# A gated mix of attention and a token MLP: the first layer's row work in a written order, other places in memory, another tail

## The chip, the core and the metric

The kernel runs on one core of a Trainium2 chip. Times are device microseconds of one launch. A core has five instruction streams that matter here: TensorE (PE, matmuls; its weight loads are counted apart as PEld), VectorE (DVE), ScalarE (ACT), GpSimd (POOL) and SyncE (SP, which issues most of the DMAs). Engines wait for each other by semaphores only; each of them runs its own instructions in order.

## The reference

The inputs are x (1 x 2048 x 512), the attention's weights, the weights and biases of a two-layer MLP that works across the tokens, and a gate's weights. All is in fp32.

```python
def _A_ref(x, wqkv, wo):                       # 32 heads of 16 columns
    qkv = (x @ wqkv).reshape(B, S, 3, H, Dh) ...
    scores = jnp.einsum("bhqd,bhkd->bhqk", q, k) * scale
    p = _softmax(scores, axis=-1)
    o = jnp.einsum("bhqk,bhkd->bhqd", p, v)
    return (o, heads side by side) @ wo

def _B_ref(x, w1, b1, w2, b2):
    h = _layernorm(x, axis=-1)                 # (B, S, D)
    u = _gelu(jnp.einsum("bsd,sf->bdf", h, w1) + b1)
    y = jnp.einsum("bdf,fs->bds", u, w2) + b2
    return y transposed to (B, S, D)

g = _sigmoid((x * gate_w).sum(-1, keepdims=True))
return g * _A_ref(x, wqkv, wo) + (1 - g) * _B_ref(x, w1, b1, w2, b2)
```

## The kernel before

Every fp32 operand of a matmul is split into two parts, hi and lo, in a faster matmul format (`split`, L65 and L66: a copy makes hi, a subtraction makes lo), and a product is three matmuls: hi with hi, hi with lo, lo with hi. Rows of x are taken in 16 chunks of 128, counted by c or t.

The work goes in these stages, in times of the profiled execution:

- To 53 us: x is loaded and turned (its transpose is kept as xt_hi and xt_lo), V and the gate are computed. The weights wv of V are four tiles, each with its hi and lo.
- To 145 us: the Q and K projections. Their split results go to DRAM as `qp` and `kp`. The first eight row chunks are normalised beside them (`ln_load`, `ln_scale`, `ln_rows`), which gives half 0 of h, `h_hi` and `h_lo` for c = 0 to 7.
- 145 to 306 us: the MLP's first layer (`layer`, L370). It has four passes over columns of w1, from f0 = 0, 512, 1024 and 1536; each of the first three fills four PSUM banks, the last fills two. In each pass, chunk after chunk, a weight block of 128 x 512 is loaded (`w_raw`, SP), split (`w_hi` on ACT, `w_lo` on POOL), and used by twelve matmuls. In the pass with f0 = 0, the layernorm of chunks 8 to 15 (half 1 of h) runs beside the first eight chunks. When a pass is done, its banks go through `gelu` (L378 to L383 and the split L65, L66), which uses the buffers `gu` and `gs` (two of each) and writes `u_hi` and `u_lo`.
- 307.6 to 314.5 us: the first 30 matmuls of the MLP's second layer (L696) into the bank `dn`.
- 314.6 to 1305.4 us: attention in 32 groups (two heads by half of the rows of Q each). A group's K and Q go by `load_k` into one of two fixed buffers, ks0 and ks1, and by `load_q` into `qs` (six and eight DMAs on SP, L424). Scores (L711) go to PSUM banks `s`, ACT exponentiates them (L720), and their products with V are summed in the bank `av` (L675). The rest of the second layer and most of the output projection are matmuls placed between these by a list written out by hand (L749). The four rows of each of K's buffers that carry a constant are filled once, by four memsets on DVE (L415).
- From 1305.4 us: the tail. The last group's output is divided by its softmax sums and goes into the projection of the last eight row chunks, and their rows are finished and stored.

Up to the attention a scheduler orders the instructions of each engine, by dependences and its own estimates, except in stretches under `manual_schedule`, where the order is that of the program. From the second layer's first matmul on, all engines are in program order.

Tiles lie in pools that are stacked from the left or the right side of SBUF. When a pool is closed, its bytes can be given out again; the first writer of the new tile then waits for the last reader of the old one. So where a pool stands in the stack decides who waits for whom. `k_bufs` (ks0, ks1) and `qs` are opened on the left after h and the first layer's pools have closed. PSUM has eight banks of 128 x 512 fp32: two for each of the three `s` buffers, one for `dn`, one for `av`.

Of the kernel before, what the change touches and what calls it, by code (L numbers as in the profile page):

```python
# [21 lines left out]
P = 128  # L22
# [36 lines left out]
def gated_mix(ctx: ExitStack, tc: tile.TileContext, a_x, a_wqkv, a_wo, b_w1, b_b1, b_w2, b_b2, gate_w, out):  # L59
# [81 lines left out]
    def weight():  # L141
        load_weight()
        split_weight()
        return ready.pop(0)
# [17 lines left out]
    with tc.tile_pool(name="vp", bufs=1, side="right") as pool:  # L162
# [104 lines left out]
    def ln_load(ln, c):  # L267
        xs[c] = ln.tile([P, D], F32, name="x")
        nc.sync.dma_start(xs[c], xf[c * P : (c + 1) * P, :])
        nc.vector.bn_stats(stats[:, c, :], xs[c])  # L270
        nc.vector.bn_aggr(mv[:, c, :], stats[:, c, :])

# [17 lines left out]
        split(h_hi[c], h_lo[c], hf, nc.scalar.copy, nc.vector.tensor_tensor)  # L290


    h_half(0)
    bd = h_ctx.enter_context(tc.tile_pool(name="bd", bufs=2))
    with tc.tile_pool(name="ln0", bufs=3, side="right") as ln:

# [17 lines left out]
        for b in range(ND):  # L314
# [9 lines left out]
            for n in range(NQ):  # L324
                ps = project(wq_b, n)
                parts(ps, qp_d[b], n, kmax[:, 0:1])
                greatest(qmax[:, n : n + 1], ps)
                if n % 2 and qk_cols:
                    qk_w.append(wcols(qk_cols.pop(0)))
                if n % 2 == 0:  # L330
                    c = 2 * b + n // 2
                    ln_load(ln, c)
                    ln_scale(ln, c, 1)
# [12 lines left out]
    def bring_most():  # L346
        nc.sync.dma_start(most_d, most)
        nc.sync.dma_start(most_row, most_d.rearrange("p b -> (p b)")[None, :])
# [23 lines left out]
    with tc.tile_pool(name="ln1", bufs=3, side="right") as ln, tc.tile_pool(name="gl", bufs=2, side="right") as gl:  # L372

        def gelu(ps, fb):
# [115 lines left out]

    end_ctx = ExitStack()
    end = sums_of = None
    rows = {}

    def open_end():
# [18 lines left out]
        slow.append((two + 5, lambda: split(wq[0], wq[1], raw, nc.vector.tensor_copy, nc.vector.tensor_tensor)))  # L514

    def fetch_o(half, k, pairs=4):

# [113 lines left out]

    two = 0

    def evacuate(g):
# [141 lines left out]
    with (  # L776
# [13 lines left out]
        sums, hi, lo = ([x.rearrange("p (i m c) -> p m i c", i=2, m=2)[:, m] for m in range(2)] for x in tiles)  # L790
        totals, last = (x.rearrange("p (i m c) -> p m i c", i=2, m=2) for x in (pa[7], last_ot))
        for m in range(2):
            nc.vector.tensor_scalar_max(sums[m], totals[:, m], LEAST_SUM)
        for m in range(2):
            nc.vector.reciprocal(sums[m], sums[m])  # L795
# [3 lines left out]
        behind = []  # L799
        for m in range(2):  # L800
            for i in range(2):
                for n, (a, b) in enumerate(((hi, 0), (hi, 1), (lo, 0))):
                    for j in range(4):
                        at = slice(32 * j, 32 * j + DH)
                        nc.tensor.matmul(pa[2 * j + m], a[m][at, i, :], wq[b][at, i, :], start=False, stop=i == 1 and n == 2)
            if m == 0:
                others(5, 7)
            for j in range(4):
                t = 2 * j + m
                row, gate, dst = rows[NH + t], g[:, NH + t : NH + t + 1], of[(NH + t) * P : (NH + t + 1) * P, :]  # L810
                if j == 1 or j == 3 and m == 0:
                    res = end.tile([P, D], F32, name=f"res{t}")
                    nc.scalar.activation(res, pa[t], AF.Copy, scale=gate)
                    nc.gpsimd.tensor_tensor(row, res, row, ALU.add)
                    behind.append((dst, row))
                else:
                    nc.vector.scalar_tensor_tensor(row, pa[t], gate, row, ALU.mult, ALU.add)
                    nc.sync.dma_start(dst, row)
        for dst, row in behind:
            nc.scalar.dma_start(dst, row)  # L820
    end_ctx.close()
    att_ctx.close()

# [79 lines left out]
```

## Time and profile before

| | |
|---|---|
| median of 3 runs | 1328.74 us (1327.55 to 1329.35) |
| the profiled execution's own time | 1328.09 us |
| its span, first to last instruction | 1326.2 us |
| mean granted TensorE clock | 0.997 |
| TensorE busy | 1309.7 us, 99% of the span |
| ACT busy | 1095.7 us, 83% |
| DVE busy | 414.3 us, 31% |
| GpSimd busy | 202.0 us, 15% |
| moved by DMA | 138.41 MB, 104 GB/s |

How to read it: the time runs from launch to end, the span from the first to the last instruction of the profiled execution, so 1.9 us lie outside the span. Busy shares are averages over stages with different limits. In the lines that follow, a tile's name stands for all of its buffers; "out<-in" names what an instruction writes and reads; Ln is a line of the kernel before; what stands in brackets is the idle time of the engine just before the instruction, and whom the profile takes to have ended it.

### The profile page before, as it was taken

The page shows a single profiled execution, that of the slowest core. Times are in us where ns is not written, and L with a number is a line of the kernel's source. Part 1 is how long each engine was busy: PE and PEld are TensorE (multiplying, and loading weights), DVE is VectorE, ACT ScalarE, POOL GpSimd, SP SyncE. Part 2 cuts the span into 40 slices and gives each one's busy share as a digit, 9 for nine tenths or more (in the row PEclk, how much of TensorE's full clock was granted, in tenths as well). Part 3 has the DMA queues.
Part 4 walks back from the last instruction along what each step waited for, and adds up shares of the span by engine and source line. Part 5 has one row for each costly group of instructions (what it writes and reads, how often), then busy time and mean ns, then how long its engine had stood idle before and what let it go on. Part 6 is the DMA issues. An engine that isn't in the chain of part 4 may idle for free.

```text
span 1326.2 us, 32411 instructions
## 1 busy us (share of the span) xinstructions
PE 1309.7 (99%) x13284; PEld 767.8 (58%) x13284; DVE 414.3 (31%) x626; ACT 1095.7 (83%) x1264; POOL 202.0 (15%) x468
## 2 busy tenths in 40 slices
PE   9999999999999999999999999999999999999996
PEld 7888878876555555555555555455554555545553
DVE  3596572445121111112422111232111112233224
ACT  3344343446999999999999999999999999999993
POOL 0210244442111111011100111100010101100001
PEclk9999999999999999999999999999999999999998
DMA  3588543328343333344555344544433433465411
GB/s 120 167 271 298 201 120 96 95 66 173 74 85 65 61 74 73 65 80 76 132 117 122 79 73 77 118 113 117 77 66 61 81 62 77 82 117 123 103 53 67
DMA packets 93385, 138.41 MB, mean 104 GB/s; under 512 B 14293, under 2 KB 53355, under 8 KB 90156
## 3 DMA queue, kind: packets, MB, share of 16 engines
q1 hardware_dynamic: 92796, 135.47, 43.4%
q8 instruction: 107, 1.75, 0.6%
q10 hardware_dynamic: 432, 0.79, 0.2%
q14 instruction: 50, 0.41, 0.1%
HBM read 99.63 MB, written 36.56 MB: 103 GB/s over the span
## 4 chain that ended last, share of the span: by engine, by line
PE 95%; DVE 2%; issue 1%; POOL 1%; ACT 0%; DMA 0%; SPq 0%; POOLq 0%; DVEq 0%
PE av L675 37%; PE s L711 28%; PE dn L749 10%; PE acc L73 10%; PE acc L370 9%; DVE ks L415 1%; PE dn L696 1%; PE acc L181 1%; POOL w_lo L66 1%; DMA wv_raw<-in_A_wqkv_dram 0%; DVE u_lo L66 0%; DVE sums L795 0%; DVE gs L381 0%; DVE gu L378 0%; ACT pt L720 0%
## 5 line engine op out<-in xcount | busy, mean ns | idle before, releaser
L720 ACT ACTIVATE pt<-s 128x1024 f32<-128x1024 f32 x1024 | 964.4, 1026 | 26.9 <-PE s L711 17.7
L711 PE MATMUL s<-qs,ks 64*128 64x512 f32 x2048 | 523.3, 420 | 0.5 <-ACT pt L720 0.4
L675 PE MATMUL av<-pt,v 128*17 128x256 f32 x8192 | 510.6, 381 | 0.0
L711 PEld LDWEIGHTS s<-qs,ks 64*128 64x128 f32 x2048 | 299.8, 184 | 205.6 <-ACT pt L720 179.0
L675 PEld LDWEIGHTS av<-pt,v 128*17 128x17 f32 x8192 | 205.2, 97 | 259.9 <-issue 119.5
L749 PE MATMUL dn<-u_hi,w_hi 64*128 64x512 f32 x428 | 182.1, 425 | 0.0
L66 POOL TENSOR_TENSOR w_lo<-w_raw,w_hi 128x512 fp32r<-128x512 f32 (+1 forms) x126 | 152.9, 1217 | 134.3 <-ACT w_hi L65 113.6
L749 PE MATMUL dn<-u_hi,w_lo 64*128 64x512 f32 x428 | 168.6, 394 | 0.0
L749 PE MATMUL dn<-u_lo,w_hi 64*128 64x512 f32 x428 | 168.6, 394 | 0.0
L753 POOL MEMSET token<- 1x1 f32 x320 | 30.3, 95 | 872.6 <-PE dn L749 666.4
L636 DVE COPY ot<-av 128x512 f32<-128x512 f32 x32 | 22.1, 692 | 355.2 <-PE av L675 348.6
L649 DVE RECIPROCAL rt<-rt 128x512 f32<-128x512 f32 x31 | 103.9, 3353 | 1.1
L370 PE MATMUL acc<-h_hi,w_lo 128*128 128x512 f32 x224 | 89.1, 398 | 1.9 <-POOL w_lo L66 1.8
L65 ACT CAST w_hi<-w_raw 128x512 fp32r<-128x512 f32 (+1 forms) x67 | 37.7, 565 | 64.0 <-PE acc L370 58.9
L370 PE MATMUL acc<-h_hi,w_hi 128*128 128x512 f32 x224 | 88.7, 396 | 0.4 <-ACT w_hi L65 0.4
L370 PE MATMUL acc<-h_lo,w_hi 128*128 128x512 f32 x224 | 88.5, 395 | 0.0
L749 PEld LDWEIGHTS dn<-u_hi,w_hi 64*128 64x128 f32 x428 | 78.8, 184 | 3.0
L749 PEld LDWEIGHTS dn<-u_lo,w_hi 64*128 64x128 f32 x428 | 79.2, 185 | 1.9
L749 PEld LDWEIGHTS dn<-u_hi,w_lo 64*128 64x128 f32 x428 | 79.0, 185 | 2.1
L65 DVE CAST w_hi<-w_raw 128x512 fp32r<-128x512 f32 (+1 forms) x61 | 22.4, 378 | 121.8 <-PE dn L749 59.6
L439 DVE TENSOR_SCALAR row<-dn,b2x,omg 128x512 f32<-128x512 f32 x16 | 13.0, 810 | 141.6 <-PE dn L749 133.2
L370 PEld LDWEIGHTS acc<-h_hi,w_lo 128*128 128x128 f32 x224 | 42.1, 188 | 14.1 <-POOL w_lo L66 4.1
(128 smaller groups left out, 1074.0 us busy)
## 6 DMA issues: line engine op xcount, KB each, us to landing
w_raw<-in_B_w_dram SPq DMA_DIRECT2D x96, 256.0 KB
ks<-kp SPq DMA_DIRECT2D x192, 128.0 KB
qs<-qp SPq DMA_DIRECT2D x256, 64.0 KB
qp<-pc SPq DMA_DIRECT2D x16, 768.0 KB
x<-in_A_x_dram SPq DMA_DIRECT2D x32, 256.0 KB
kp<-pc SPq DMA_DIRECT2D x16, 512.0 KB
w_raw<-in_B_w_dram SPq DMA_DIRECT2D x32, 128.0 KB
bp<-row SPq DMA_DIRECT2D x16, 256.0 KB
```

What stands on the lines that cost most here:

```text
L65: copy(hi, src)
L66: sub(lo, src, hi.bitcast(F32), ALU.subtract)
L73: nc.tensor.matmul(ps, a, b, start=start and n == 0, stop=stop and n == last)
L181: nc.tensor.transpose(pt[:, k, :], xs[t][:, k * P : (k + 1) * P], ident)
L370: nc.tensor.matmul(p, a, b, start=first and k == 0, stop=last and k == 2)
L636: nc.vector.tensor_copy(ot, av)
L649: nc.vector.reciprocal(rt, rt)
L675: nc.tensor.matmul(av[32 * j : 32 * j + VC, i * QC : (i + 1) * QC], v[:, c, g % NP * 2 + i, :], pt[:, h * QC : (h + 1) * QC], start=added[ ...
L711: nc.tensor.matmul(s[:, m, :], kt[grp][rows, c * P : (c + 1) * P], qt[grp][rows, qb * NB : (qb + 1) * NB], start=True, stop=True,)
L720: nc.scalar.activation(pt, s, AF.Exp, scale=SCALE)
L749: mm = nc.tensor.matmul(ps, a[half], b[half], start=first and not second, stop=last and bool(second))
L753: fence = nc.gpsimd.memset(token, 0.0)
```

## The change

Six things, in the order of the diff:

1. The hi and lo parts of three of the four wv tiles no longer have tiles of their own; they take the places of `w_hi` and `w_lo` (three buffers each), and the fourth takes two places of `w_raw`, which the first layer uses later.
2. `h_half` takes a side. h_lo lies ahead of h_hi in each half. Half 1 goes to the right side, below u, where it was on the left above half 0. What is opened on the right later (the x rows of the first layer and gu, gs) lies further down for it. By the compiled addresses, in bytes of a partition: half 1 of h from 118752 to 151520 (before: h_hi 87904 to 104288, h_lo 104288 to 120672); gu and gs from 95936 to 104128 (before: 132800 to 140992); ks0 from 89664 to 97856 and ks1 from 97856 to 106048 in both kernels.
3. The first pass of the first layer (f0 = 0) is under `manual_schedule` for ACT, DVE and GpSimd. `rows_beside(c)` writes out what goes beside chunk c: loads of x two chunks ahead (five buffers), the statistics of chunk 8 + c, for two chunks at a time the scale (`ln_scale` with n = 2, on odd c), and the rows of chunk 8 + c - 2.
4. The PSUM pools of attention are opened in another order: the three `s` buffers in banks 0 to 5, `dn` in 6, `av` in 7 (before: dn 0, av 1, s 2 to 7).
5. The last group's output is taken from `av` by two max operations with a value per partition, `least`, so that the sums can't be zero; the max against LEAST_SUM behind the sums' matmul goes.
6. In the tail, the sums are two matmuls of half the columns, the reciprocals read PSUM, the copy for hi of the first half is ACT's, the order of the matmuls of the other groups changes (2, 4, 6; 1; 3, 7, 5), and rows t = 0 and 4 (DVE, stored by SP) and 2 and 6 (ACT and GpSimd, stored from ACT's queue) are finished ahead of or beside the second half's matmuls; then 3 (ACT and GpSimd) and 1, 5, 7 (DVE, SP).

```diff
-            wv.append((raw, pool.tile([P, D], F32R, name=f"wv_hi{k}"), pool.tile([P, D], F32R, name=f"wv_lo{k}")))
+            names = ("w_hi", "w_lo") if k < 3 else ("w_raw", "w_raw")
+            wv.append((raw, *(wk.tile([P, D], F32R, name=n, bufs=4 if n == "w_raw" else 3) for n in names)))
...
-    def h_half(lo):
-        h_pool = h_ctx.enter_context(tc.tile_pool(name=f"h{lo}", bufs=1))
+    def h_half(lo, side):
+        h_pool = h_ctx.enter_context(tc.tile_pool(name=f"h{lo}", bufs=1, side=side))
+        lo_t = h_pool.tile([P, NH, D], F32R, name="h_lo")
         hi_t = h_pool.tile([P, NH, D], F32R, name="h_hi")
-        lo_t = h_pool.tile([P, NH, D], F32R, name="h_lo")
...
-    h_half(NH)
     u_pool = u_ctx.enter_context(tc.tile_pool(name="u", bufs=1, side="right"))
     u_hi = u_pool.tile([P, NF, D], F32R, name="u_hi")
     u_lo = u_pool.tile([P, NF, D], F32R, name="u_lo")
+    h_half(NH, "right")
...
+        def rows_beside(c):
+            if c == 0:
+                bring_most()
+                for n in range(2):
+                    ln_load(ln, NH + n, 5)
+            if c + 2 < NH:
+                ln_load(ln, NH + c + 2, 5)
+            if 2 <= c < NH + 2:
+                ln_rows(ln, NH + c - 2)
+            if c < NH:
+                ln_stats(NH + c)
+                if c % 2:
+                    ln_scale(ln, NH + c - 1, 2)
+            if c == NH + 4:
+                least_shifts()
+
+        beside = {mybir.EngineType.Activation, mybir.EngineType.DVE, mybir.EngineType.Pool}
...
-            for c in cs:
-                if f0 == 0 and c < NH:
-                    ln_load(ln, NH + c)
-                    ln_scale(ln, NH + c, 1)
-                    ln_rows(ln, NH + c)
-                hi, lo = weight()
-                layer(ps, hi, lo, (h_hi[c], h_lo[c]), c == cs[0], c == cs[-1])
-                if f0 == 0 and c == 0:
-                    bring_most()
-                if f0 == 0 and c == NH:
-                    least_shifts()
+            with tc.manual_schedule(engines=beside) if f0 == 0 else ExitStack():
+                for c in cs:
+                    hi, lo = weight()
+                    if f0 == 0:
+                        rows_beside(c)
+                    layer(ps, hi, lo, (h_hi[c], h_lo[c]), c == cs[0], c == cs[-1])
...
+    ps_s = psum_ctx.enter_context(tc.tile_pool(name="ps_s", bufs=3, space=PSUM, reuse_waits="tile"))
     ps_dn = psum_ctx.enter_context(tc.tile_pool(name="ps_dn", bufs=1, space=PSUM, reuse_waits="tile"))
     ps_av = psum_ctx.enter_context(tc.tile_pool(name="ps_av", bufs=1, space=PSUM, reuse_waits="tile"))
-    ps_s = psum_ctx.enter_context(tc.tile_pool(name="ps_s", bufs=3, space=PSUM, reuse_waits="tile"))
...
+        if g == NG - 1:
+            for x, y in zip(column_halves(ot), column_halves(av)):
+                nc.vector.tensor_scalar_max(x, y, least[0])
+            return ot
         nc.vector.tensor_copy(ot, av)
-        if g == NG - 1:
-            return ot
...
-        nc.tensor.matmul(pa[7], sums_of, last_ot, start=True, stop=True)
...
+        totals = column_halves(pa[5])
         for m in range(2):
-            nc.vector.tensor_scalar_max(sums[m], totals[:, m], LEAST_SUM)
-        for m in range(2):
-            nc.vector.reciprocal(sums[m], sums[m])
-            nc.vector.tensor_mul(sums[m], last[:, m], sums[m])
-            split(hi[m], lo[m], sums[m], nc.vector.tensor_copy, nc.vector.tensor_tensor)
-        others(2, 4, 6, 1, 3)
...
+            nc.tensor.matmul(totals[m], sums_of, last[m], start=True, stop=True)
+        others(2, 4, 6)
...
+        nc.vector.reciprocal(sums[0], totals[0])
+        nc.vector.tensor_mul(sums[0], last[0], sums[0])
+        nc.scalar.copy(hi[0], sums[0])
+        nc.vector.reciprocal(sums[1], totals[1])
+        low(0)
+        nc.vector.tensor_mul(sums[1], last[1], sums[1])
+        nc.vector.tensor_copy(hi[1], sums[1])
+        low(1)
...
+        last_pair(0, [(hi, 0, False), (hi, 1, False)])
+        others(1)
+        last_pair(0, [(lo, 0, True)])
+        others(3, 7, 5)
+        for t in (2, 6):
+            scaled(t)
+        for t in (0, 4):
+            finish(t)
+        last_pair(1, [(hi, 0, False), (hi, 1, False), (lo, 0, True)])
+        for t in (2, 6):
+            store(t)
+        scaled(3)
+        for t in (1, 5, 7):
+            finish(t)
+        store(3)
```

More of the change, by code (lines that the diff above doesn't have):

```diff
@@ L290, in ln_rows @@
         split(h_hi[c], h_lo[c], hf, nc.scalar.copy, nc.vector.tensor_tensor)
-    h_half(0)
+    h_half(0, "left")
     bd = h_ctx.enter_context(tc.tile_pool(name="bd", bufs=2))
@@ L332, in gated_mix @@
                     ln_load(ln, c)
+                    ln_stats(c)
                     ln_scale(ln, c, 1)
@@ L492, in gated_mix @@
     end = sums_of = None
+    least = []
     rows = {}
@@ L514, in open_end @@
         slow.append((two + 5, lambda: split(wq[0], wq[1], raw, nc.vector.tensor_copy, nc.vector.tensor_tensor)))
+        least.append(end.tile([P, 1], F32, name="least"))
+        nc.vector.tensor_reduce(least[0], ident.rearrange("p (j r) -> p j r", r=32)[:, :, DH], axis=AX.X, op=ALU.add)
+        nc.vector.tensor_scalar(least[0], least[0], -1.0, 3e38, ALU.add, ALU.mult)
+        nc.vector.tensor_scalar_add(least[0], least[0], LEAST_SUM)
     def fetch_o(half, k, pairs=4):
@@ L632, in gated_mix, with column_halves @@
     two = 0
+    def column_halves(x):
+        x = x.rearrange("p (i m c) -> p m i c", i=2, m=2)
+        return x[:, 0], x[:, 1]
     def evacuate(g):
         ot = out_pool.tile([P, NB], F32, name="ot")
+        if g == NG - 1:
+            for x, y in zip(column_halves(ot), column_halves(av)):
+                nc.vector.tensor_scalar_max(x, y, least[0])
+            return ot
         nc.vector.tensor_copy(ot, av)
-        if g == NG - 1:
-            return ot
         half, p = divmod(g, NP)
@@ L787, in gated_mix @@
         others(0)
-        nc.tensor.matmul(pa[7], sums_of, last_ot, start=True, stop=True)
         tiles = [end.tile([P, NB], dt, name=name) for name, dt in (("sums", F32), ("hi", F32R), ("lo", F32R))]
-        sums, hi, lo = ([x.rearrange("p (i m c) -> p m i c", i=2, m=2)[:, m] for m in range(2)] for x in tiles)
-        totals, last = (x.rearrange("p (i m c) -> p m i c", i=2, m=2) for x in (pa[7], last_ot))
+        sums, hi, lo = (column_halves(x) for x in tiles)
+        last = column_halves(last_ot)
@@ L792, in gated_mix @@
+        totals = column_halves(pa[5])
         for m in range(2):
-            nc.vector.tensor_scalar_max(sums[m], totals[:, m], LEAST_SUM)
-        for m in range(2):
-            nc.vector.reciprocal(sums[m], sums[m])
-            nc.vector.tensor_mul(sums[m], last[:, m], sums[m])
-            split(hi[m], lo[m], sums[m], nc.vector.tensor_copy, nc.vector.tensor_tensor)
-        others(2, 4, 6, 1, 3)
[L799 to L802, printed above, removed]
+            nc.tensor.matmul(totals[m], sums_of, last[m], start=True, stop=True)
@@ new lines, in gated_mix, with low, last_pair @@
+        others(2, 4, 6)
+        def low(m):
+            nc.vector.tensor_tensor(lo[m], sums[m], hi[m].bitcast(F32), ALU.subtract)
+        nc.vector.reciprocal(sums[0], totals[0])
[6 more added lines that the diff above has]
+        low(1)
+        def last_pair(m, parts):
+            for a, b, end_of in parts:
+                for i in range(2):
@@ L803, in gated_mix @@
                     for j in range(4):
                         at = slice(32 * j, 32 * j + DH)
[L805 to L818, printed above, removed]
@@ L819, in gated_mix, with row_of, finish @@
-        for dst, row in behind:
-            nc.scalar.dma_start(dst, row)
+                        nc.tensor.matmul(
+                            pa[2 * j + m], a[m][at, i, :], wq[b][at, i, :], start=False, stop=end_of and i == 1
+                        )
+        def row_of(t):
+            return rows[NH + t], g[:, NH + t : NH + t + 1], of[(NH + t) * P : (NH + t + 1) * P, :]
+        def finish(t):
+            row, gate, dst = row_of(t)
+            nc.vector.scalar_tensor_tensor(row, pa[t], gate, row, ALU.mult, ALU.add)
+            nc.sync.dma_start(dst, row)
@@ new lines, in scaled, with store @@
+        def scaled(t):
+            res = end.tile([P, D], F32, name=f"res{t}")
+            nc.scalar.activation(res, pa[t], AF.Copy, scale=row_of(t)[1])
+            nc.gpsimd.tensor_tensor(row_of(t)[0], res, row_of(t)[0], ALU.add)
+        def store(t):
+            nc.scalar.dma_start(row_of(t)[2], row_of(t)[0])
+        last_pair(0, [(hi, 0, False), (hi, 1, False)])
[4 more added lines that the diff above has]
+            scaled(t)
```

5 lines of the change are left out of this document (3 added, 2 removed).

## The prediction

> **What bounds the kernel now.** I read the page's engine table and slices first, then busy time by stage, then the stage borders instruction by instruction.
>
> ```profile
> PE 1309.7 (99%) x13284; PEld 767.8 (58%) x13284; DVE 414.3 (31%) x626; ACT 1095.7 (83%) x1264; POOL 202.0 (15%) x468
> ```
>
> ```profile
> 140.00:180.00 40.00, 38.59 (x164) 30.02 (x163) 27.46 (x89) 14.14 (x29) 12.52 (x9) 1.00 0.58 185
> 180.00:210.00 30.00, 29.37 (x126) 23.13 (x125) 17.78 (x25) 16.39 (x27) 16.21 (x12) 1.00 0.34 98
> 210.00:240.00 30.00, 30.00 (x130) 24.16 (x129) 3.40 (x6) 8.61 (x14) 13.72 (x11) 1.00 0.36 104
> ```
>
> ```profile
> 300.00:320.00 20.00, 18.29 (x102) 12.97 (x104) 14.18 (x18) 10.84 (x17) 6.89 (x8) 1.00 0.76 173
> 320.00:1300.00 980.00, 980.00 (x11749) 509.65 (x11743) 221.82 (x229) 955.26 (x1016) 100.61 (x377) 1.00 0.43 87
> 1300.00:1327.00 27.00, 15.83 (x149) 8.89 (x145) 12.12 (x17) 6.47 (x8) 4.11 (x4) 0.86 0.23 82
> ```
>
> The window rows give the stretch, its length, then busy time (and instructions) of PE, its weight loads, DVE, ACT and POOL, the granted clock, the DMA share and GB/s. TensorE is the bound: 1309.7 of 1326.2 us, and in the 980 us of attention it never idles. ACT is busy for 955.26 of those 980, so attention has no slack in which a late start is made up; a microsecond lost before 320 us is a microsecond at the end. What an edit of the schedule can win is PE's idle time alone: 1.41 + 0.63 = 2.04 us in 140 to 210 (the first layer's first pass), 1.71 in 300 to 320 (the border to attention), and 11.2 in the tail.
>
> The change adds and removes almost no matmul work, so every term below is idle time of PE at one of these three places, or the end of the last store.
>
> **Border to attention, the largest term.** These rows are of the timeline: start, duration, engine, line, operation, and in brackets idle time before it and its releaser.
>
> ```profile
> 296.99 0.38 SPq L424 DMA_DIRECT2D ks<-kp  x1
> 304.25 1.76 DVE L415 MEMSET ks<- 16x2048 f32 x1 [0.46 <-issue]
> 305.61 5.74 SPq L424 DMA_DIRECT2D qs<-qp  x8
> 307.61 0.47 PE L696 MATMUL dn<-u_hi,w_hi 128*128 128x512 f32 x1 [1.20 <-ACT gs L379]
> 312.57 0.68 DVE L66 TENSOR_TENSOR u_lo<-gu,u_hi 128x512 fp32r<-128x512 f32 x1
> 314.28 0.39 PE L696 MATMUL dn<-u_hi,w_lo 128*128 128x512 f32 x1
> 314.60 0.50 PE L711 MATMUL s<-qs,ks 64*128 64x512 f32 x1
> ```
>
> In the kernel before, the first K loads start at 296.99, the four constant fills of the K buffers end at 306.01 (the last is 304.25 + 1.76), and the Q loads are issued by 311.35. So K and Q lie ready when PE ends its 30 second-layer matmuls, and the first score matmul follows at 314.60 after 0.3 us.
>
> In the changed kernel half 1 of h leaves the left side for the right, and the gelu's buffers gu and gs move down the stack with it: gu's first buffer now lies from byte 95936 of a partition, ks0 from 89664 to 97856, and ks1 covers the rest of gu and gs. In the kernel before, ks0 and ks1 lay over a part of h that was read for the last time some 10 us before layer 1 ended. Now the first K load and the fills wait for the last reader of gu: the u_lo of block 12, which can't begin before layer 1's last matmul. That is the row at 312.57: it ends at 313.25. SP issues in order, so the other five K loads, the eight Q loads and the three weight loads behind them wait as well; on DVE the four fills (7 us) come behind it, and the weight splits of attention behind those.
>
> What the loads then take is read where they run almost alone, late in attention:
>
> ```profile
> 974.24 2.74 SPq L424 DMA_DIRECT2D ks<-kp  x6
> ```
>
> ```profile
> GB/s 8 0 25 94 12 524 0 197 328 229 295 0 0 197 197 131 0 0 229 295 0 0 164 295 66 0 4 51 105 104 135 113 45 0 0 0 66 0 0 0
> ```
>
> The second row cuts 974 to 984 us into 40 slices of 0.25 us. From the first issue at 974.24 the transfers end in slice 33, at 982.2: 8.0 us for six K loads of 128 KB, with a few small ones beside them. The first score matmul waits for three K and four Q loads, but the Q loads are issued behind all six K loads. Four Q loads are 0.25 MB against the 0.77 MB of K, so at the same rate another 8.0/3 = 2.7 us; some of that is start-up paid already, so I take 1.5. First score at 313.25 + 8.0 + 1.5 = 322.8 instead of 314.60: **+8.2 us**. The new place of dn (bank 6, no longer the one that the last gelu still reads) takes away the 1.20 us at 307.61, and PE finishes the 30 matmuls at about 313.4; that only lengthens the wait that follows and wins nothing. Bounds: the second fill of ks0 ends 313.25 + 0.68 (the other u_lo) + 2 x 1.76 = 317.5, so if the transfers took no longer, +2.9; with all 2.7 us for Q and half a microsecond to start, +9.9.
>
> **The clock.** That wait leaves PE idle for 9.4 us, from 313.4 to 322.8. Nothing like it stands in the trace but the end:
>
> ```profile
> 1315.71 0.41 PE L805 MATMUL pa<-wq,lo 16*128 16x512 f32 x4
> ```
>
> ```profile
> 1316.20:1319.40 3.20, 0.00 (x0) 0.00 (x0) 2.01 (x3) 0.69 (x1) 1.27 (x1) 1.00 0.91 316
> 1319.40:1326.00 6.60, 0.00 (x0) 0.00 (x0) 0.00 (x0) 0.00 (x0) 0.00 (x0) 0.50 0.50 181
> ```
>
> PE's last matmul ends at 1316.1 (the row with four of them), and from 1319.4 on, 3.3 us later, the clock granted is 0.50. So attention would start at half speed. How long it stays there no row shows. At least nothing; and if the clock came back after as long a time of work as it took to fall, 3.3 us at half speed would cost 1.7. I take **+1.2**, range 0 to 1.7. The Trainium skill, "TensorE: Matmul & The Clock Gate", Part 1, says the same of both directions: half rate after an idle window of about 3.4 us, and full rate after about as long a time of work; by it the cost would be an estimated 1.7 us, or less where ACT limits the first scores anyway.
>
> **First pass in program order.** From the first layer's first pass:
>
> ```profile
> 145.29 0.40 PE L370 MATMUL acc<-h_hi,w_hi 128*128 128x512 f32 x1
> 156.72 0.69 DVE L270 BATCH_NORM_STATS2 stats<-x 128x6 f32<-128x512 f32 x1 [8.04 <-PE acc L370]
> 158.78 0.20 ACT L279 ACTIVATE y<-w 128x1 f32<-128x1 f32 x1 [4.50 <-DVE far L355]
> 158.89 0.60 ACT L65 CAST w_hi<-w_raw 128x512 fp32r<-128x512 f32 x1
> 159.57 1.30 POOL L66 TENSOR_TENSOR w_lo<-w_raw,w_hi 128x512 fp32r<-128x512 f32 x1 [3.92 <-ACT w_hi L65]
> 161.33 0.55 DVE L289 TENSOR_SCALAR hf<-x,mv,rs 128x512 f32<-128x512 f32 x1
> 161.91 0.62 ACT L65 CAST h_hi<-hf 128x512 fp32r<-128x512 f32 x1 [0.45 <-DVE hf L289]
> 163.01 0.69 DVE L66 TENSOR_TENSOR h_lo<-hf,h_hi 128x512 fp32r<-128x512 f32 x1
> 163.13 3.50 POOL L66 TENSOR_TENSOR w_lo<-w_raw,w_hi 128x512 fp32r<-128x512 f32 x2 [2.26 <-ACT w_hi L65]
> 163.62 1.26 DVE L285 TENSOR_TENSOR rs<-y,t 128x1 f32<-128x1 f32 x1
> ```
>
> ```profile
> L66 DVE TENSOR_TENSOR h_lo<-hf,h_hi 128x512 fp32r<-128x512 f32 x8 | 6.2, 770 | 0.5 <-ACT h_hi L65 0.3
> L285 DVE TENSOR_TENSOR rs<-y,t 128x1 f32<-128x1 f32 x8 | 3.2, 405 | 0.0
> L271 DVE BATCH_NORM_AGGREGATE mv<-stats 128x2 f32<-128x6 f32 x8 | 1.4, 172 | 0.1
> L280 DVE RECIPROCAL y<-y 128x1 f32<-128x1 f32 x8 | 1.2, 156 | 0.0
> ```
>
> PE takes 30.00/130 = 0.231 us for a matmul (window 210 to 240), 2.77 for a chunk of twelve, 5.5 for two. Now the engines beside it go strictly in the written order, and the weight splits, which PE needs every 2.77 us, stand in ACT's queue between the layernorm's steps. Per two chunks DVE does two each of hf 0.55, h_lo 0.69, stats 0.69 and aggregate 0.17, 4.2 us, and waits twice for h_hi (0.62); then one scale chain: w, five small operations of about 0.16 and the 0.20 of y on ACT, 1.2 us. That is 6.6 us, and hand-overs between DVE and ACT, eight of them at the 0.03 from the end of hf (161.88) to h_hi (161.91), make it 6.9. Beside POOL's split it is longer: rs takes 1.26 at 163.62, in the middle of POOL's 3.50 for two splits that alone take 1.30 each, and its mean over the eight rows is 405 ns against the 156 of a reciprocal of the same size. So 0.25 for rs and as much again for each of the two other small operations with two inputs, and 0.08 for each h_lo (mean 770 against 690): 0.9 per pair, **7.8 us per two chunks against PE's 5.5**. The worst is one collision in full in each chain, 1.1 as at 163.62, and the same for h_lo: 8.2. The Trainium skill, "SBUF — State Buffer", Who interferes with whom, gives the reason (DVE with two SBUF inputs and a GpSimd instruction that reads SBUF share a port pair, held by one for a whole instruction); by it a collision costs what is left of the split, so a pair stays below 6.9 + 1.3 for each collision, which the 1.1 of the row agrees with.
>
> What comes of it: y of the first two rows can't be earlier than in the trace, 158.78, since the loads of x are no earlier. Behind it on ACT comes the split for c = 5, and behind each later y the ones for c = 7, 9 and 11. The one for c = 11 is ready at 158.78 + 3 x 7.8 + 0.6 + 1.3 = 184.1, and PE without idling needs it at 145.3 (its first matmul of the layer) + 11 x 2.77 + 2 x 0.23 = 176.2 or so. It is 7.9 late; that is the sum of PE's idle time in the pass. Against 2.04 now: **+5.8**. At 6.9 a pair it is 181.4, +3.2; at 8.2 and with the splits of the last two rows late by another 1.0, +8.1. Below nothing it can come too: if ACT keeps up, all of the 2.04 goes.
>
> **The places of wv** make the first three weight splits wait for the end of the V stage, near 52 us, and they are used from 145 us on: nothing.
>
> **Tail.**
>
> ```profile
> 1304.32 1.03 PE L675 MATMUL av<-pt,v 128*17 128x256 f32 x12
> 1308.00 1.74 DVE L795 RECIPROCAL sums<-sums 128x256 f32<-128x256 f32 x1
> 1314.78 3.43 DVE L817 SCALAR_TENSOR_TENSOR base<-pa,g,base 128x512 f32<-128x512 f32 x5
> 1315.55 4.50 SPq L818 DMA_DIRECT2D out_dram<-base  x5
> 1316.32 3.22 ACTq L820 DMA_DIRECT2D out_dram<-base  x3
> ```
>
> ```profile
> GB/s 0 0 0 0 0 0 0 0 0 0 0 158 339 339 399 361 339 126 382 333 360 383 377 382 393 361 382 169 153 49 22 27 0 22 22 0 0 0 0 0
> ```
>
> Of the DMA slices (0.375 us from 1312) the stores run from 1316.1 to 1324.4 at up to 399 GB/s, eight stores issued within 1315.55 to 1320.05. The change drops the max against the least sum (two operations, 0.4 us each), turns the copy of the last group into two max operations of the same sort, reads the sums from PSUM, puts one copy on ACT, and stores four rows before the second half's matmuls. By hand from the end of the last attention matmul (1304.32 + 1.03): first reciprocal from +2.0 to +3.75, second to +5.95, the first half's matmuls to about +7, its stores issued from +8.3 to +10.5 instead of from +10.2, the second half's from +11.5 to +13, the last landing 2.5 to 3 after its issue, at about +16, against +19.1 (1324.4) now. **-3.0**, range -0.5 to -3.5.
>
> **Sum**, against the profiled execution's 1328.1 (its span of 1326.2 and 1.9 around it; the median of three, 1328.7, is 0.6 above): 1328.1 + 8.2 + 1.2 + 5.8 - 3.0 = **1340.3 us**.
>
> **Rivals.**
> First, the pass keeps up: ACT's queue holds no split long enough, the 2.04 us go, and the border alone counts: 1328.1 - 2.0 + 8.2 + 1.2 - 3.0 = 1332.5. For it: ACT is busy for only 14.14 of 40 us there. Against it: the 6.9 us chain is of dependent steps, not of busy time. It is a slower case too.
> Second, on the other side: the K and Q loads are not what starts attention. If they were issued as now, at 297, PE would go on at 313.4 instead of 314.6, the border would win 1.2, and with the tail's 3.0 and the pass's 2.0 the time is 1328.1 - 6.2 = 1321.9. It decides at the landing of the fourth Q load: before 314.6 the border costs nothing. Against it stand the addresses: a load into bytes that a gelu still reads can't go.
> Third, small terms: loads and fills at the lower bound (+2.9), no cold clock, a pass that keeps up, and the tail's 3.0: 1328.1 + 2.9 - 2.0 - 3.0 = 1326.0, near no change.
> Fourth, all at their worst: 1328.1 + 9.9 + 1.7 + 8.1 - 0.5 = 1347.3.
>
> **Numbers.** A measurement of this kernel tells 0.2%, 2.7 us, from no change. My forecast (pass late and border late) has 0.55, the first rival 0.20, the fourth 0.07, the second 0.10, the third 0.08. Slower: 0.55 + 0.20 + 0.07 = 0.82, less 0.02 for the first rival's low edge: 0.80. The third is split: 0.04 within and 0.04 faster; with the first rival's 0.02, same is 0.06 and faster 0.14. The range goes from 1327.0, which leaves out the faster cases, to 1347.5; my forecast's own is 1336 (the pass at +3.2, no cold clock, the tail at -3.5) to 1347.
>
> **What would show it.** Right: the first ks load issued at about the end of layer 1 + 6.8 us, PE idle for 8 to 10 us ahead of the first score with a DMA of qs as releaser, a clock below 1 just after it, some 7 us of PE idle in the first pass put down to w_lo or w_hi, and a last store about 16 us behind attention. Wrong: ks loads before the layer's end, or a pass without idle time.

## The result and the profile after

The changed kernel takes 1343.5 us (median of five runs, 1341.74 to 1346.07) against 1328.74 us: a ratio of 1.0115, interval 1.0099 to 1.0131. The forecast was 1340.3 us, and slower. The profiled execution is the slowest of the five, 1346.07 us, and stands 18.0 above that of the kernel before; the median stands 14.8 above. Over the five runs the mean granted clock goes down as the time goes up, from 0.993 at 1341.74 us to 0.989 at 1346.07.

The page's engine rows, and the windows of the same stretches as before (320 to 340 apart):

```profile
PE 1316.4 (98%) x13286; PEld 772.9 (58%) x13286; DVE 411.8 (31%) x603; ACT 1095.8 (82%) x1261; POOL 198.1 (15%) x468
```

```profile
140.00:180.00 40.00, 35.97 (x148) 26.77 (x147) 22.27 (x49) 12.10 (x23) 8.97 (x7) 1.00 0.54 176
180.00:210.00 30.00, 27.68 (x117) 21.20 (x116) 20.98 (x37) 14.43 (x26) 14.26 (x11) 1.00 0.35 99
...
320.00:340.00 20.00, 11.28 (x92) 7.10 (x94) 7.17 (x6) 8.50 (x10) 0.26 (x3) 0.66 1.06 153
340.00:1300.00 960.00, 960.00 (x11520) 498.12 (x11518) 217.61 (x227) 936.46 (x995) 98.76 (x371) 1.00 0.42 86
```

TensorE's idle time in 140 to 210 us has grown from 2.04 to 6.35, and there is a hole of almost nine in 320 to 340, at a clock of 0.66. The rest of attention has none, as before. What TensorE waited for between 140 and 340 us, in the view of waits:

```profile
PE s L741 <- DMA qs<-qp: 10.0, 1, 10.0
PE acc L375 <- POOL w_lo L66: 3.9, 9, 0.6
PE acc L375 <- ACT w_hi L65: 2.6, 3, 0.9
```

The border in the timeline:

```profile
311.51 0.40 PE L375 MATMUL acc<-h_hi,w_lo 128*128 128x512 f32 x1
317.23 1.28 DVE L66 TENSOR_TENSOR u_lo<-gu,u_hi 128x512 fp32r<-128x512 f32 x2
317.94 2.65 SPq L442 DMA_DIRECT2D ks<-kp  x6
318.36 0.39 PE L726 MATMUL dn<-u_hi,w_lo 128*128 128x512 f32 x1
320.63 6.29 SPq L442 DMA_DIRECT2D qs<-qp  x8
328.72 0.76 PE L741 MATMUL s<-qs,ks 64*128 64x512 f32 x1 [9.97 <-DMA qs<-qp]
```

The first K load goes the moment the first of the two u_lo is done (317.94), 6.0 us behind the end of layer 1's last matmul (311.51 + 0.40), and TensorE, done with its 30 matmuls at 318.75, waits for the fourth Q load until 328.72. It then starts at half speed: a score matmul of 0.76 us where it was 0.50.

The two profiles by stage (first matmul of layer 1; start of its last; first score; end of the last attention matmul, 1318.57 + 2.56 = 1321.13; end of the span):

| stage | before, us | after, us | more | forecast |
|---|---|---|---|---|
| to layer 1 | 145.29 | 146.21 | 0.9 | 0 |
| layer 1 | 160.7 | 165.3 | 4.6 | 5.8 |
| border to the first score | 8.6 | 17.2 | 8.6 | 8.2 |
| attention | 990.75 | 992.4 | 1.7 | 1.2 |
| tail | 20.85 | 22.8 | 1.9 | -3.0 |

### The profile page after: what moved, and what is told of

Its sections match the earlier page's. It is cut to its first block, busy times and chain, and to the rows that moved or that the text cites. A ratio compares the mean times of both kernels' runs of the same rounds, so it can differ in the third digit from the quotient of the medians.

```text
span 1343.9 us, 32400 instructions
## 1 busy us (share of the span) xinstructions
PE 1316.4 (98%) x13286; PEld 772.9 (58%) x13286; DVE 411.8 (31%) x603; ACT 1095.8 (82%) x1261; POOL 198.1 (15%) x468
## 4 chain that ended last, share of the span: by engine, by line
PE 95%; issue 2%; POOL 1%; DMA 1%; DVE 1%; ACT 0%; SPq 0%; POOLq 0%; ACTq 0%
PE av L705 36%; PE s L741 28%; PE acc L73 10%; PE dn L779 10%; PE acc L375 9%; POOL w_lo L66 1%; PE acc L183 1%; PE pa L815 0%; DMA qs<-qp 0%; PE pa L844 0%; DMA ks<-kp 0%; PE acc L217 0%; DMA w_raw<-in_B_w_dram 0%; DVE sums L830 0%; DVE base L853 0%
## 5 line engine op out<-in xcount | busy, mean ns | idle before, releaser
L66 POOL TENSOR_TENSOR w_lo<-w_raw,w_hi 128x512 fp32r<-128x512 f32 (+1 forms) x126 | 149.5, 1189 | 142.5 <-ACT w_hi L65 122.8
```

Source lines behind the costliest of these rows:

```text
L66: sub(lo, src, hi.bitcast(F32), ALU.subtract)
```

## The experiments

### Four rows of x instead of five

```diff
-                    ln_load(ln, NH + n, 5)
+                    ln_load(ln, NH + n, 4)
-                ln_load(ln, NH + c + 2, 5)
+                ln_load(ln, NH + c + 2, 4)
```

> The changed kernel with four buffers for the rows of x in the first layer instead of five. gu and gs then lie 2048 bytes higher, from 97984, above ks0 (which ends at 97856); ks1 still lies under them. Theory (the places in memory make the border wait): the K loads need no gelu any more and go when SP comes to them, at about 309; the fills of ks0 are still behind the last gelu on DVE, so the first score comes at about 321 instead of 328.7, and PE idles for 2 us instead of 10, too short for the clock to fall: 7.9 + 1.7 less, about 1334 us. Rival (the wait comes from the new bank order or from the written order of the first pass): no change, 1343.5 us, and the wait for qs stays at 10 us.

Measured: 1334.16 us, 1.0043 of before (1.0028 to 1.0059). 2048 bytes in the stack are worth 9.3 us. The border in its timeline:

```profile
308.30 2.77 SPq L442 DMA_DIRECT2D ks<-kp  x6
316.08 3.55 SPq L442 DMA_DIRECT2D qs<-qp  x8
318.07 1.76 DVE L433 MEMSET ks<- 16x2048 f32 x1 [0.48 <-issue]
320.05 0.46 PE L741 MATMUL s<-qs,ks 64*128 64x512 f32 x1 [2.22 <-DMA qs<-qp]
```

The K loads are free from 308.30. What remains are the fill (319.83) and the Q loads, which now start at 316.08: the second gs has moved up with the rest, to 104128 + 2048, and lies 128 bytes into the first Q buffer, which I hadn't seen. So the theory holds, and the size came out right with a second cause in it. The rival, banks or order, falls. One part of the expectation was wrong: the wait of 2.2 us was not too short for the clock to fall. In the 3.4 us ahead of the fall TensorE was busy for 1.18 us, and then it ran at about half clock for 3.4:

```profile
317.20:320.60 3.40, 1.18 (x8) 0.74 (x8) 2.44 (x3) 0.00 (x0) 0.00 (x0) 1.00 0.55 153
320.60:324.00 3.40, 3.40 (x17) 2.44 (x15) 2.92 (x2) 3.22 (x4) 0.09 (x1) 0.53 0.91 254
```

Attention takes 991.2 us here, 0.45 more than before. The profile of the changed kernel also has a tail of 22.8 us against 20.65 here, so the two spans stand 12.0 apart, where the border and the start of attention make 7.8 and 1.2.

### The places alone

The kernel before with half 1 on the right and five buffers for x:

```diff
-    h_half(NH)
...
+    h_half(NH, "right")
...
-                    ln_load(ln, NH + c)
+                    ln_load(ln, NH + c, 5)
```

> The kernel before with half 1 of h on the right side and five buffers for x in the first layer, nothing else. Theory (places alone make the border wait): border +8.8 and clock +1.7, the first pass as before: about 1339 us, with a wait of some 9 us for qs ahead of the first score. Rival (the order of the first pass or the banks make it): 1328.7 us.

Measured: 1338.93 us, 1.0076 (1.006 to 1.0091). Two of TensorE's waits between 140 and 340 us:

```profile
PE s L711 <- DMA qs<-qp: 8.8, 1, 8.8
PE dn L696 <- DVE gu L378: 0.9, 1, 0.9
```

The places do it, with only the buffers for x beside them. Attention takes 994.5 us there, 3.7 more than before, and its first 5.9 us are at half clock. What that costs shows where the first matmuls of `av` start, first in the kernel before, then in this one:

```profile
318.94 1.49 PE L675 MATMUL av<-pt,v 128*17 128x256 f32 x24
```

```profile
327.91 1.49 PE L675 MATMUL av<-pt,v 128*17 128x256 f32 x24
```

They come 4.34 us behind the first score in the kernel before and 5.97 here, so the half clock has 1.6 of the 3.7. The other 2.1 build up in small steps over the later groups, at full clock; what makes them isn't traced.

### The first pass left to the scheduler

```diff
-        beside = {mybir.EngineType.Activation, mybir.EngineType.DVE, mybir.EngineType.Pool}
-            with tc.manual_schedule(engines=beside) if f0 == 0 else ExitStack():
...
+                if f0 == 0 and c < NH:
+                    ln_load(ln, NH + c, 5)
+                    ln_stats(NH + c)
+                    ln_scale(ln, NH + c, 1)
+                    ln_rows(ln, NH + c)
```

> The changed kernel, but the first layer's first pass as in the kernel before: no written order, one row at a time; memory, banks and tail stay as changed. Theory (the written order costs the pass): the first layer takes 161.1 us as before instead of 165.5, so 4.4 less: about 1339 us, with about 2 us of PE idle time in the pass. Rival (the pass is late because of the new places of h and x): no change, 1343.5 us, PE idle time of 6.3 us as in the changed kernel.

Measured: 1334.89 us, 1.0055 (1.004 to 1.0071), 8.6 less than the changed kernel where 4.4 were expected. From its first matmul to the first of dn, the first layer takes 158.2 us here, 165.5 in the changed kernel and 161.1 in the kernel before (162.3 less the wait of 1.2). So the written order costs 7.4 us, and the new places give 2.9 back. The rival, the new places of h and x, falls. Of the 11.6 us between the two profiles' spans, 1.2 more are the start of attention (991.2 us), where the half clock covers 3.1 us instead of 6.0, and 2.4 the tail (20.4), where in this profile the clock doesn't fall while there is work.

What the places give back shows in the two stretches from the first matmul of chunk 8 to the first of the next pass, in the pass f0 = 512, 96 matmuls in each; first of before, then of the changed kernel:

```profile
216.04:238.44 22.40, 22.40 (x98) 18.02 (x97) 1.88 (x3) 6.02 (x10) 10.36 (x8) 1.00 0.33 95
```

```profile
222.70:244.50 21.80, 21.80 (x97) 18.02 (x96) 1.82 (x3) 5.98 (x10) 10.32 (x8) 1.00 0.35 97
```

No idle time in either, and 22.40/96 = 233 ns a matmul against 21.80/96 = 227. Half 1 is read by 336 matmuls of the layer: 2.0 us.

### ACT out of the written order

```diff
-        beside = {mybir.EngineType.Activation, mybir.EngineType.DVE, mybir.EngineType.Pool}
+        beside = {mybir.EngineType.DVE, mybir.EngineType.Pool}
```

> The changed kernel, in which the first layer's first pass is in written order on DVE and GpSimd only; ACT is left to the scheduler. Theory (the weight splits wait in ACT's queue behind the layernorm's steps): the first layer takes about 159 us instead of 165.5, and the time is about 1337 us. Rival (DVE's own order makes the pass late, through its collisions with GpSimd and late rows): 165 us and 1343.5 us.

Measured: 1334.69 us, 1.0042 (1.0026 to 1.0057), 2.3 below what was expected; the first layer takes 157.2 us, 8.3 less than in the changed kernel and a microsecond less than when the scheduler has all three engines. Its tail, 20.8 us in the profile against 22.8, has a part in the time. ACT in the changed kernel's timeline:

```profile
159.76 0.20 ACT L283 ACTIVATE y<-w 128x2 f32<-128x2 f32 x1 [7.36 <-DMA x<-in_A_x_dram]
159.87 0.60 ACT L65 CAST w_hi<-w_raw 128x512 fp32r<-128x512 f32 x1
...
167.88 0.20 ACT L283 ACTIVATE y<-w 128x2 f32<-128x2 f32 x1 [1.78 <-DVE w L282]
167.99 0.60 ACT L65 CAST w_hi<-w_raw 128x512 fp32r<-128x512 f32 x1
...
176.00 0.20 ACT L283 ACTIVATE y<-w 128x2 f32<-128x2 f32 x1 [1.78 <-DVE w L282]
```

and in this kernel:

```profile
157.35 0.62 ACT L65 CAST w_hi<-w_raw 128x512 fp32r<-128x512 f32 x1 [2.23 <-PE acc L375]
159.40 0.20 ACT L283 ACTIVATE y<-w 128x2 f32<-128x2 f32 x1 [1.42 <-DMA x<-in_A_x_dram]
...
166.61 0.20 ACT L283 ACTIVATE y<-w 128x2 f32<-128x2 f32 x1 [1.43 <-DVE w L282]
...
174.95 0.20 ACT L283 ACTIVATE y<-w 128x2 f32<-128x2 f32 x1 [1.44 <-DVE w L282]
```

In the changed kernel ACT sits idle for 7.36 us in front of y, waiting for rows of x, with the split that TensorE wants queued behind it. Here that split runs at 157.35, ahead of y. The chain of the rows is hardly faster, 7.2 us from the first y to the second and 8.3 to the third, against 8.1 in the changed kernel, and harms little: the waits of the pass are 1.2 us. What cost the time is what was queued behind it. The rival, DVE's own order, falls.

### The clock at attention's start

```diff
+        warm = ps_s.tile([P, 2, NB], F32, name="s")
+        for n in range(42):
+            nc.tensor.matmul(warm[:, n % 2, :], a, b, start=True, stop=True)
```

> The changed kernel with 42 matmuls more on TensorE between the second layer's 30 and the first score, into a score bank, on data that lie there: work that is not needed, 9.5 us long, in the time that TensorE waits for K and Q. Theory (the half clock after the wait costs attention's start 1.7 us): the first score comes as late as before, the clock stays whole there, and attention takes 990.8 us instead of 992.4: about 1341.8 us. Rival (attention's start is bound by ACT, and the clock costs nothing there): 1343.5 us.

Measured: 1341.49 us (1339.31 to 1341.73), 2.0 less than the changed kernel. Windows of the wait and of the first scores, of the changed kernel and then of this one:

```profile
318.80:328.70 9.90, 0.00 (x0) 0.01 (x1) 7.06 (x4) 0.00 (x0) 0.00 (x0) 0.61 1.02 133
328.70:334.70 6.00, 5.98 (x24) 4.10 (x24) 1.12 (x2) 4.75 (x6) 0.09 (x1) 0.50 1.16 211
```

```profile
318.80:327.60 8.80, 8.61 (x39) 6.79 (x37) 6.41 (x4) 0.00 (x0) 0.00 (x0) 1.00 1.00 121
327.60:334.00 6.40, 5.87 (x54) 3.29 (x56) 1.12 (x2) 5.61 (x6) 0.18 (x2) 1.00 1.14 202
```

The counts of the two second rows are of different matmuls; the same work is what lies ahead of the first matmuls of `av`, again of the changed kernel and then of this one:

```profile
334.71 1.49 PE L705 MATMUL av<-pt,v 128*17 128x256 f32 x24
```

```profile
331.96 1.49 PE L705 MATMUL av<-pt,v 128*17 128x256 f32 x24
```

From the first score (328.72 and 327.66) that is 5.99 us at half clock and 4.30 at full: 1.7 less, as the theory has it. Over the whole of attention (991.06 us) 1.35 are left; the difference of 0.3 comes some 590 us later. The rival, that ACT hides it, has a share: six microseconds of half clock cost 1.7, not three.

### The banks alone

In the kernel before:

```diff
+    ps_s = psum_ctx.enter_context(tc.tile_pool(name="ps_s", bufs=3, space=PSUM, reuse_waits="tile"))
     ps_dn = psum_ctx.enter_context(tc.tile_pool(name="ps_dn", bufs=1, space=PSUM, reuse_waits="tile"))
     ps_av = psum_ctx.enter_context(tc.tile_pool(name="ps_av", bufs=1, space=PSUM, reuse_waits="tile"))
-    ps_s = psum_ctx.enter_context(tc.tile_pool(name="ps_s", bufs=3, space=PSUM, reuse_waits="tile"))
```

> The kernel before with the changed order of the PSUM banks alone. Theory (dn no longer shares a bank with the last gelu's input): the 1.2 us of idle time at 307.6 go, the first score comes at 313.4, when the last Q load has just landed: 1327.5 us. Rival (K and Q decide anyway): 1328.7 us.

Measured: 1327.61 us, 0.9989 (0.998 to 0.9998). As the theory has it: the wait for gs ahead of dn is not among TensorE's waits any more, nor is one for K or Q.

### The tail alone

The kernel before with the change's lines for `least`, `evacuate` and all behind attention:

```diff
-        others(2, 4, 6, 1, 3)
+        others(2, 4, 6)
...
+        last_pair(0, [(hi, 0, False), (hi, 1, False)])
+        others(1)
+        last_pair(0, [(lo, 0, True)])
+        others(3, 7, 5)
```

> The kernel before with the changed tail alone. By the prediction's count of the tail the time is 3.0 less, 1325.7 us, if TensorE keeps its full clock. In the changed kernel's profile the clock fell in the tail, at the matmuls of 16 rows. Theory (those matmuls and the gaps about them make the clock fall, in every run): the tail takes 22.8 us as there instead of 20.9, about 1330.6 us. Rival (it was chance, or came of the half clock earlier in that kernel): 1325.7 us.

Measured: 1329.34 us over eleven runs, 1.0003 (0.9994 to 1.0012): no difference, and neither the gain of 3.0 nor the loss of 1.9. Its profile, from the end of attention at 1305.4:

```profile
1305.40:1312.90 7.50, 6.80 (x45) 4.52 (x45) 6.18 (x10) 0.44 (x2) 0.00 (x0) 1.00 0.00 0
1312.90:1316.30 3.40, 3.40 (x9) 2.40 (x8) 1.28 (x2) 1.23 (x2) 2.51 (x2) 0.50 0.42 152
1316.30:1319.00 2.70, 1.88 (x25) 1.08 (x24) 0.78 (x2) 0.69 (x1) 0.00 (x0) 1.00 0.57 209
```

For 3.4 us the clock is half, and the tail takes 21.9 us. In the changed kernel it falls 6.9 us behind attention and doesn't come back while there is work, and the tail takes 22.8:

```profile
1321.10:1328.00 6.90, 6.19 (x43) 4.29 (x43) 5.84 (x9) 0.40 (x1) 0.00 (x0) 1.00 0.00 0
1328.00:1335.80 7.80, 7.75 (x41) 4.67 (x37) 1.65 (x4) 1.26 (x2) 2.51 (x2) 0.50 0.38 139
```

In the profiles of four other kernels with this tail (e1_four_x, e2_pass_free, e6_warm, e8_act_free) the clock holds until the last matmul, and the tail takes 20.4 to 20.8 us, against 20.8 to 21.7 for the tail of before in five profiles. So it doesn't fall in every run, against the theory, and it does fall without a half clock earlier in the kernel, against a part of the rival. That the new tail is what lets it fall isn't shown by two profiles of six against none of five. In the two profiles where the clock falls, the 3.4 us ahead of the fall hold all or most of TensorE's gap of 0.7 us at the copy of hi, the first run of 16-row matmuls and a part or all of the second; the other four have the same gap and the same runs, so which mix is enough isn't settled. The Trainium skill, "TensorE: Matmul & The Clock Gate", Part 1, says that the window over which the activity is judged, about 3.4 us, runs freely; the half-clock stretch of 3.4 us agrees with that length. That such a free phase is why some of these profiles have the fall and others not is argued, not shown.

### Three versions that keep what helps

The kernel before with half 1 on the right, the banks in the new order, and the pool of the exponentiated scores opened ahead of K's and Q's, so that these lie above gu and gs:

```diff
+    ptp = att_ctx.enter_context(tc.tile_pool(name="pt", bufs=6, reuse_waits="tile"))
     stk = att_ctx.enter_context(tc.tile_pool(name="stk", bufs=2, reuse_waits="tile"))
```

> The kernel before with three parts: half 1 of h on the right side (three buffers for x, as before), the changed order of the PSUM banks, and the pool of the exponentiated scores opened ahead of that of K and Q, so that K lies above the gelu's buffers and over bytes that are free before layer 1 ends. First pass and tail as before. Theory: matmuls that read half 1 of h come 227 instead of 233 ns apart (336 of them, -2.0), the 1.2 us ahead of dn go, and K and Q land in time: 1328.7 - 3.2 = 1325.5 us. Rival (K and Q land as late as they did, about 313.2, because SP issues them no earlier): the first score stays near 313.2 and only 1.4 us go: 1327.3 us.

Measured: 1326.14 us, 0.9979 (0.997 to 0.9988). The border is 6.9 us from the first dn matmul to the first score, 30 matmuls and no wait.

Then the written order on DVE and GpSimd (`rows_beside` as in the change):

```diff
+        beside = {mybir.EngineType.DVE, mybir.EngineType.Pool}
+            with tc.manual_schedule(engines=beside) if f0 == 0 else ExitStack():
```

> The version e5_best (half 1 of h on the right, changed banks, K and Q above the gelu's buffers, tail of before) with the changed kernel's written order for the first pass on DVE and GpSimd, ACT left to the scheduler. Theory (the written order of the rows is good, only ACT's is not): the first layer takes 157.2 us as in e8_act_free instead of 159.1, so 1.9 less than e5_best: about 1324.2 us. Rival (the gain of e8_act_free belongs to its other places for x or wv): 1326.1 us.

Measured: 1323.99 us, 0.9962 (0.9949 to 0.9976), and a first layer of 157.2 us, as said. Last the changed tail with another order of its matmuls:

```diff
-        others(2, 4, 6)
+        others(2, 4, 6, 1)
...
-        last_pair(0, [(hi, 0, False), (hi, 1, False)])
-        others(1)
-        last_pair(0, [(lo, 0, True)])
+        last_pair(0, [(hi, 0, False), (hi, 1, False), (lo, 0, True)])
```

> e9_order_dve_pool with the changed tail, in which the matmuls of row t = 1 go ahead of the first 16-row matmuls, so that TensorE has no gap at the copy of hi and the 16-row matmuls of the first half go in one run. Theory (the half clock in the tail needs the gap of 0.7 us and the work of few rows in one window of 3.4 us): the clock stays whole until the last matmul and the tail takes 20.0 us, 0.8 less than that of before: about 1323.4 us. Rival (few rows alone let the clock fall): the tail takes 21.5 to 22.8 us: 1325 to 1326 us.

Measured: 1323.3 us, 0.9953 (0.9939 to 0.9966), the fastest of all; its five runs (at most 1323.73) all lie below the five of the one before it (at least 1323.82), by 0.7 us in the median. In its profile TensorE is at full clock, and busy but for 0.26 us, to the end of its work:

```profile
1301.70:1306.00 4.30, 4.30 (x23) 3.39 (x19) 3.31 (x5) 0.16 (x1) 0.00 (x0) 1.00 0.00 0
1306.00:1312.40 6.40, 6.14 (x59) 3.70 (x57) 4.06 (x7) 1.51 (x3) 2.54 (x2) 1.00 0.25 91
```

and the tail takes 19.9 us. One profile isn't proof that the clock never falls in it.

## Why the prediction was right, and where it was not

**Border: right, +8.6 for +8.2.** The mechanism is shown from both sides: places alone bring the wait, 2048 bytes take most of it away (10.0 us to 2.2). The release was 6.0 us behind the layer's end against the 6.8 reckoned, and the loads took 10.8 from the first issue to the first score where the sum had 9.5, so two misses cancel in part. The lower bound named the second fill of ks0. The first score needs only the first: in the version with four rows it starts at 320.05, when the second fill (320.32) has not begun.

**Clock: right, +1.7 for +1.2.** The warm version takes it away. The length was mis-sized, the half clock lasted 6.0 us behind the first score where 3.3 were put, but not all of it costs time. The range of 0 to 1.7 holds: the places alone lost 1.6 at this point, three other kernels 0.5, 0.5 and 1.0.

**First pass: right in kind, with a part missed.** The pair takes 8.12 us (159.76, 167.88, 176.00) where 7.8 was reckoned, since the collision with GpSimd hits in full in each pair. The first of them, and the groups of DVE in the pass, after:

```profile
160.55 1.27 POOL L66 TENSOR_TENSOR w_lo<-w_raw,w_hi 128x512 fp32r<-128x512 f32 x1 [6.78 <-ACT w_hi L65]
160.59 1.25 DVE L288 TENSOR_SCALAR t<-t 128x2 f32<-128x2 f32 x1
```

```profile
L288 DVE TENSOR_SCALAR t<-t 128x2 f32<-128x2 f32 x4 | 5.1, 1263 | 0.1
L289 DVE TENSOR_TENSOR rs<-y,t 128x2 f32<-128x2 f32 x4 | 0.6, 161 | 0.1
```

It is the tensor_scalar that stands for 1.1 us in all four pairs, and the operations with two inputs beside it are not slowed. So the rate was about right and the operation wrong: the argument that three two-input operations lose 0.25 each was a mean over hits and misses. The cost of the order is 7.4 us by the layer's length, not 5.8; the layer's net 4.6 is near the forecast because the places gave 2.0 back at half 1, which I had not seen, and the scheduler's pass idles somewhat less in the new places. And idle time undercounts a stop: the waits of the pass add to 6.5 us in the changed kernel and to 1.2 in the version with ACT free, but the layer is 8.3 shorter. Each stop also loses the overlap of two matmuls, 0.39 long and 0.23 apart, and the next one comes 0.34 behind the first instead of 0.23. That is about 0.28 a stop; for the nine stops more (twelve against three) it makes an estimated 2.5 of the 3.0 that the waits leave out.

**Tail: wrong, +1.9 for -3.0.** Two steps failed. The landing "2.5 to 3 after its issue" was too short: with the whole clock the changed tail starts its last issue about where the sum had it (+13.4 for +13), but the span ends 6.7 behind the end of that issue. In these rows, of the version with the pass left to the scheduler, attention ends at 1311.89 and the span at 1332.3:

```profile
1320.04 5.55 SPq L842 DMA_DIRECT2D out_dram<-base  x5
```

```profile
1325.26 0.37 ACTq L850 DMA_DIRECT2D out_dram<-base  x1
```

Nearly the same distance stood in the trace of before, 6.2 from 1320.05 to 1326.2: 4.35 to the last transfer (1324.4), where I put 2.5 to 3 for the new order, and 1.8 more to the end of the span. So the last issue ends 1.0 us sooner behind attention (13.7 for 14.7), its landing takes 0.5 longer, and the new order is worth 0.4 us in this profile (20.4 against 20.85), not 3.0. The other step is one that wasn't there: that TensorE's clock could fall in the middle of the tail, at gaps below a microsecond. It has the other 2.4 (22.8 against 20.4).

**The start: +0.9, not forecast.** The first matmuls run slow for a while, and for how long differs between profiles. The same matmul in before and after, some 8 us in:

```profile
7.57 0.40 PE L73 MATMUL acc<-wv_hi,xt_lo 128*128 128x512 f32 x1
```

```profile
8.06 0.63 PE L73 MATMUL acc<-w_hi,xt_lo 128*128 128x512 f32 x1
```

The views give a granted clock of 1.00 for both there, so a slow clock as the reason isn't shown. Over the twelve profiles layer 1 starts at 145.2 to 147.0, with the places of wv old or new, so it isn't charged to the change.

**The sum.** By the table the terms missed by +0.9, -1.2, +0.4, +0.5 and +4.9 us, 5.5 together. The medians stand 14.8 apart and the two profiles 18.0, and that hides 3.2 of it: that the forecast lies within 3.2 us of the median is in part luck. The first rival, a pass that keeps up, falls with the 6.5 us of waits for the splits, and the second, loads that go as before, with the first K load at 317.94.

## What to carry to other kernels

When a pool moves, compare the addresses of what is opened later over the same bytes: the first writer inherits the last reader, and 2 KB of stack decided 9 us here. A written order for an engine is only as good as the slowest producer ahead of each instruction in its queue; leave out of it the engine that feeds the bottleneck. Putting the feed first might do as well; no run here shows it. And read the end of the last store from the distance between last issue and end that the trace already shows.

## What the hardware showed that I had not expected

Matmuls that read half 1 of h come 227 ns apart from its new place and 233 from its old, with the same weights' buffers and no idle time; half 0 reads at 233 in both kernels. The version with the places alone, where h_hi lies ahead of h_lo as before, has 227 too (48 matmuls from 215.94 to 226.86). Why wasn't settled: it may be the place in SBUF or the distance to something else that is read.

TensorE's clock fell to a half behind a stretch of 3.4 us that holds a gap of 0.7 us and 16-row matmuls, and in another kernel behind a wait of 2.2 us, where I had thought it takes a wait of 3.3. Across the profiles a half clock at the start of attention cost between 0.5 and 1.7 us, the more the longer it went on behind the first score: 0.5 for 3.1 and 3.4 us, 1.0 for 4.5, 1.6 and 1.7 for 5.9 and 6.0.

A tensor_scalar of 128x2 elements beside GpSimd's split took 1263 ns, four times of four, against 161 for its neighbours. The Trainium skill, "SBUF — State Buffer", Who interferes with whom, lists tensor_scalar among the operations that can take the shared ports; the row agrees.
